# Pooled attention and a squared-ReLU MLP on one core: the attention's score eviction, its normalisation and its query pooling are dealt out anew over ScalarE, VectorE and GpSimd

## The chip, the core and the metric

The kernel runs on one core of one Trainium2 chip. The metric is device time in microseconds (us) of one execution, as the median of several. Five engines work side by side and meet at semaphores: TensorE (PE in the profile; its weight loads are PEld), VectorE (DVE), ScalarE (ACT), GpSimd (POOL) and SyncE (SP, which only issues DMAs here). Each works through its own list of instructions in order.

## The reference

```
q, k, v: (4, 8, 1152, 64) float32;  w_in: (512, 2048);  w_out: (2048, 512)
q_pool = q.reshape(B, H, 576, 2, 64).mean(axis=3)
scores = q_pool @ k.T / 8
scores = scores - max(scores, axis=-1)
attn   = exp(scores);  attn = attn / (sum(attn, axis=-1) + 1e-9)
x      = (attn @ v) with heads side by side: (2304, 512)
h      = maximum(x @ w_in, 0)
out    = (h * h) @ w_out
```

## The kernel before

**Attention.** There are 32 heads, worked on as 16 pairs `n`; a pair is cut into two halves `e` of 288 pooled queries (`NH`). One (pair, half) is the unit of work. Its scores are computed transposed, in nine chunks `c` of 128 keys (`scores`, six matmuls a chunk, into a PSUM buffer `s` of two banks). VectorE moves each chunk to SBUF and takes its maximum on the way (`evict`, L355). After the ninth chunk the nine maxima become one per partition (`max_fin`, `pb`, L309), TensorE transposes them (`max_turn`), and VectorE reduces again (`max_rows`, `nb`, L325). ScalarE then takes the exponential in place, three chunks to an instruction (`expo`, L360); a group of three chunks is a tile `p`. GpSimd adds the three tiles, and then the three chunks of the result, so that one chunk is left (`add`, L397: two adds of 1728 elements a partition and two of 576). TensorE sums that over the keys with a matmul by ones (`total`, L404) and multiplies the exponentials by v (`pv`, L375), both into the one PSUM buffer `c` of the pool `cps`. ScalarE copies the sums out (`total_x`, L408), VectorE inverts them (`recip`, L414), ScalarE sums the inverses up for a later check of the range (`spread`, L417), and VectorE multiplies (`pv_x`, L420) into `xt`.

Before a pair's scores stand its loads, the pooling of its queries on GpSimd (`pool_q`, L225 and L227), transposes of k and q on TensorE in four steps `u` (`prep`), and the split of each result in a high part on ScalarE (`prep_high`, L268) and a low part on VectorE (`prep_low`, L273 and L275). PSUM is a ring `sps` of three buffers for scores, transposes and maxima, and `cps`.

**Order.** `plan` gives each piece of work a key from the tables `AT` and `BT` (kept above what it must follow) and sorts by key. The sorted list is the program order of every engine. While the exponentials of one half run, TensorE works on the scores of the next, and on the sums and values of the half before.

**MLP.** The weights come as pairs of 32-bit integers and are turned into float32 by six VectorE instructions (`convert`, L119 to L133), one add on GpSimd (L135) and a split (`split_w`). A weight unit `u` is one block of `w_in` (even) or `w_out` (odd). Units 0 and 1 are converted near the start, 2 and 3 at the end of the attention (`CU` is 4), the rest within the MLP. `split_x` splits tiles of x, `layer1` and `layer2` are the two matmuls; both follow the attention on TensorE.

Of the kernel before, what the change touches and what calls it, by code (L numbers as in the profile page):

```python
# [37 lines left out]
def kernel(  # L38
# [36 lines left out]
    def run(ctx, exact):  # L75
# [89 lines left out]
        with ExitStack() as a:  # L165
# [5 lines left out]
            sps = a.enter_context(tc.tile_pool(name="sps", bufs=3, space=PSUM))  # L171
            cps = a.enter_context(tc.tile_pool(name="cps", bufs=1, space=PSUM))
# [16 lines left out]
            else:  # L189
                PM = [kq.tile([P, 2, NC], F32, name=f"pm{i}") for i in range(2)]  # L190
# [167 lines left out]
            def expo(n, e, g):  # L358
                p = p_[n, e, g]
                nc.scalar.activation(out=p, in_=p, func=ACTF.Exp, bias=NB_[n % 2][:, e:e + 1])  # L360
# [6 lines left out]
            def both(n, e):  # L367
                if (n, e) not in c_:
                    c_[n, e] = cps.tile([P, 2, 512], F32, tag="c", name="c")
                return c_[n, e]  # L370

            def pv(n, e, c):
                t = both(n, e)
                for h in range(2):
                    i = nc.tensor.matmul(out=t[rows(h), 0, :NH], lhsT=ld_["v", n][:, h, c, :],  # L375
                                         rhs=chunk(n, e, c)[:, h], start=(c == 0), stop=(c == NC - 1))
                    if (n, e) in tx_:

                        tc.declare_no_dep(i.ins, tx_[n, e].ins, reason="the sums' bank is read, this writes the other bank")
# [5 lines left out]
            def parts(n, e):  # L385
                return LASTN if (n, e) == LAST else 1
# [19 lines left out]
            def total_x(n, e):  # L406
                r_[n, e] = ld.tile([P, NH], F32, tag="r", name="r", bufs=2)
                tx_[n, e] = nc.scalar.activation(out=r_[n, e], in_=c_[n, e][:, 1, :NH], func=ACTF.Copy,  # L408
                                                 bias=1e-9 if exact else 1e-30, scale=1.0 if exact else 1.0 + 1e-9,
                                                 accum_out=RM[:, 0, 2 * n + e:2 * n + e + 1])  # L410
# [5 lines left out]
            def spread(n, e):  # L416
                nc.scalar.activation(out=JK, in_=r_[n, e], func=ACTF.Copy, accum_out=RM[:, 1, 2 * n + e:2 * n + e + 1])  # L417
# [289 lines left out]
```

## Time and profile before

| | |
|---|---|
| median of 3 runs | 831.65 us (831.32 to 832.45) |
| the profiled execution | 829.95 us, its span 828.1 us |
| busy in the span | PE 765.0, DVE 596.3, ACT 429.8, POOL 455.4 us |
| busy share | PE 92%, DVE 72%, ACT 52%, POOL 55% |
| chain that ended last | PE 47%, POOL 35%, DVE 9%, issue 6% |

An engine's share is its busy time over the whole span. The attention takes roughly the first half and the MLP the second, with other engines busy in each, so the shares of the whole run don't name the limit of either half. A row of the timeline gives start, duration, engine, line, operation, and what is written from what; in square brackets stands how long the engine sat idle before it, and what ended that.

### The profile page before, as it was taken

To read this page: it belongs to the slowest core of one execution; us is meant where nothing else is said; L and a number is where in the kernel's file an instruction comes from. 1 tells how busy PE (TensorE), PEld (TensorE's weight loads), DVE (VectorE), ACT (ScalarE), POOL (GpSimd) and SP (SyncE) were. 2 spreads that over 40 slices of the span, in tenths; PEclk is the share of its full clock that TensorE was granted. 3 is DMA by queue.
4 is the path that set the end of the run, shared out by engine and by line. 5 is a ranking of instruction groups with operands and counts; after the bars stand their busy time and mean duration, and the time that the engine had idled before them with its cause. 6 is when DMAs were issued, how large, how long until landed. Compare 5 with 4: busy or idle time off the path is not lost.

```text
span 828.1 us, 13837 instructions
## 1 busy us (share of the span) xinstructions
PE 765.0 (92%) x5366; PEld 558.6 (67%) x5366; DVE 596.3 (72%) x1215; ACT 429.8 (52%) x636; POOL 455.4 (55%) x225
## 2 busy tenths in 40 slices
PE   4899999999999999997698999999999999999996
PEld 3665556555555556553476878888888888888885
DVE  5998988888888888885888699685555745445323
ACT  1565566566565566555455745454435444445431
POOL 2699999999999999999245234222112121110000
PEclk9999999999999999998899999999999999999999
DMA  9223323332223323120022112101111010000113
GB/s 246 63 58 87 86 60 87 86 87 60 76 67 87 86 63 83 30 81 0 27 77 76 52 52 77 51 28 50 51 35 42 27 46 31 1 2 26 51 52 105
DMA packets 62090, 50.78 MB, mean 61 GB/s; under 512 B 39232, under 2 KB 49472, under 8 KB 62016
## 3 DMA queue, kind: packets, MB, share of 16 engines
q1 hardware_dynamic: 60576, 47.46, 20.4%
q10 hardware_dynamic: 1440, 2.36, 0.9%
q8 instruction: 44, 0.72, 0.4%
q14 instruction: 30, 0.25, 0.1%
HBM read 45.09 MB, written 4.72 MB: 60 GB/s over the span
## 4 chain that ended last, share of the span: by engine, by line
PE 47%; POOL 35%; DVE 9%; issue 6%; ACT 1%; DMA 1%; SPq 1%; POOLq 0%; DVEq 0%; ACTq 0%
POOL ts L397 31%; PE o L614 22%; PE h L578 20%; PE c L375 3%; POOL qp L225 2%; DVE p L355 2%; PE s L344 2%; DVE xlo L158 1%; DVE h L127 1%; DVE a L124 1%; DVE r L133 1%; DMA raw<-in_moe_w_in_dram 1%; POOL r L135 1%; POOL ql L227 1%; DVE gl L586 1%
## 5 line engine op out<-in xcount | busy, mean ns | idle before, releaser
L355 DVE TENSOR_SCALAR_CACHE_REDUCE p<-s 128x576 f32<-128x576 f32 x288 | 205.0, 754 | 20.6 <-PE s L344 19.0
L578 PE MATMUL h<-xhi,wi 128*128 128x512 f32 (+1 forms) x600 | 174.1, 375 | 5.9 <-ACT wi L145 5.7
L360 ACT ACTIVATE p<-p,nb 128x1728 f32<-128x1728 f32 x96 | 159.8, 1728 | 27.9 <-DVE nb L325 27.9
L614 PE MATMUL o<-wo,gh 128*128 128x512 f32 x540 | 169.7, 395 | 0.9 <-DVE part L622 0.9
L375 PE MATMUL c<-p,vt 128*64 128x288 f32 x1152 | 169.1, 418 | 0.7 <-DVE xt L420 0.7
L344 PE MATMUL s<-qq,kk 64*128 64x288 f32 x1728 | 157.5, 315 | 9.9 <-DVE p L355 7.8
L135 POOL TENSOR_TENSOR r<-r,h 128x512 f32<-128x512 f32 x32 | 47.0, 1470 | 212.7 <-DVE r L133 212.7
L344 PEld LDWEIGHTS s<-qq,kk 64*128 64x128 f32 x1728 | 124.6, 191 | 58.2 <-DVE p L355 30.0
L578 PEld LDWEIGHTS h<-xhi,wi 128*128 128x128 f32 x600 | 110.6, 190 | 29.1 <-ACT wi L145 5.9
L397 POOL TENSOR_TENSOR ts<-p 128x1728 f32<-128x1728 f32 x32 | 123.5, 3859 | 8.0 <-ACT p L360 8.0
L397 POOL TENSOR_TENSOR ts<-ts,p 128x1728 f32<-128x1728 f32 x32 | 125.0, 3908 | 2.5
L586 DVE TENSOR_TENSOR gl<-g,gh 128x512 fp32r<-128x512 f32 (+1 forms) x80 | 54.0, 675 | 96.9 <-ACT gh L585 96.6
L614 PEld LDWEIGHTS o<-wo,gh 128*128 128x128 f32 x540 | 100.3, 188 | 24.5 <-issue 1.3
L578 PE MATMUL h<-xlo,wi 128*128 128x512 f32 (+1 forms) x300 | 111.6, 372 | 0.0
L375 PEld LDWEIGHTS c<-p,vt 128*64 128x64 f32 x1152 | 74.6, 137 | 53.7 <-issue 16.2
L614 PE MATMUL o<-wo,gl 128*128 128x512 f32 x270 | 106.6, 395 | 0.0
L397 POOL TENSOR_TENSOR ts<-ts 128x576 f32<-128x576 f32 x63 | 89.3, 1418 | 4.9
L158 DVE TENSOR_TENSOR xlo<-xt,xhi 128x1024 fp32r<-128x1024 f32 (+7 forms) x40 | 59.3, 1495 | 32.3 <-ACT xhi L157 28.8
L414 DVE RECIPROCAL r<-r 128x144 f32<-128x144 f32 x64 | 64.8, 1035 | 23.3 <-ACT r L408 23.3
L580 ACT ACTIVATE r<-h 128x512 f32<-128x512 f32 (+1 forms) x80 | 44.3, 554 | 71.0 <-PE h L578 71.0
L585 ACT CAST gh<-g 128x512 fp32r<-128x512 f32 (+1 forms) x80 | 46.3, 579 | 54.4 <-PE o L614 48.7
L622 DVE TENSOR_TENSOR part<-part,o 128x512 f32<-128x512 f32 x72 | 48.7, 686 | 21.8 <-PE o L614 21.2
(73 smaller groups left out, 759.3 us busy)
## 6 DMA issues: line engine op xcount, KB each, us to landing
kt<-in_k_dram SPq DMA_DIRECT2D x32, 288.0 KB, 4.1
vt<-in_v_dram SPq DMA_DIRECT2D x16, 576.0 KB, 3.9
qt<-in_q_dram SPq DMA_DIRECT2D x16, 512.0 KB, 3.9
raw<-in_moe_w_in_dram SPq DMA_DIRECT2D x16, 512.0 KB, 3.8
raw<-in_moe_w_out_dram SPq DMA_DIRECT2D x16, 512.0 KB, 3.3
out_dram<-part ACTq DMA_DIRECT2D x18, 128.0 KB, 3.3
out_dram<-part SPq DMA_DIRECT2D x18, 128.0 KB, 2.8
ql<-in_q_dram SPq DMA_DIRECT2D x16, 64.0 KB, 3.7
```

What stands on the lines that cost most here:

```text
L135: nc.gpsimd.tensor_tensor(out=r, in0=r, in1=h.bitcast(F32), op=ALU.add)
L158: nc.vector.tensor_tensor(out=l, in0=x, in1=h, op=ALU.subtract)
L344: nc.tensor.matmul(out=s[:, h, :NH], lhsT=l[rows(h)], rhs=r[rows(h)], start=(i == 0), stop=(i == len(terms) - 1))
L355: nc.vector.tensor_scalar(out=room(n, e, c), in0=s_.pop((n, e, c))[:, :, :NH], scalar1=1.0, scalar2=None, op0=ALU.mult, op1=ALU.max, accum ...
L360: nc.scalar.activation(out=p, in_=p, func=ACTF.Exp, bias=NB_[n % 2][:, e:e + 1])
L375: i = nc.tensor.matmul(out=t[rows(h), 0, :NH], lhsT=ld_["v", n][:, h, c, :], rhs=chunk(n, e, c)[:, h], start=(c == 0), stop=(c == NC - 1))
L397: nc.gpsimd.tensor_tensor(out=t[:, o], in0=t[:, o] if x is None else p_[n, e, x], in1=t[:, y] if isinstance(y, slice) else p_[n, e, y], op ...
L414: nc.vector.reciprocal(out=x, in_=x)
L578: nc.tensor.matmul(out=h, lhsT=w, rhs=x, start=(m == 0), stop=(m == len(mm) - 1))
L586: nc.vector.tensor_tensor(out=gl, in0=g, in1=gh, op=ALU.subtract)
L614: nc.tensor.matmul(out=acc[i][t], lhsT=g, rhs=w, start=(first and m == 0), stop=(last and m == 2))
L622: nc.vector.tensor_tensor(out=y, in0=y, in1=acc[i][t], op=ALU.add)
```

## The change

- Of the nine chunks, 3, 4 and 5 (one tile `p`) are copied out of PSUM by ScalarE. Their maximum is taken by one VectorE reduction over the tile in SBUF (`max_copied`). The chunks run in the order 0, 3, 1, 4, 2, 5, 6, 7, 8.
- The exponential of a tile is two instructions of 864 elements in place of one of 1728.
- All PSUM use of the attention is one ring of four buffers; `c` is taken from it.
- The sums are inverted as exp(-ln(sum)) on ScalarE, with one Newton step of two VectorE instructions, the first of which writes over the sums in PSUM. `recip` and `spread` are gone; a third ScalarE instruction reads the sums for the range check.
- The second half of each pair leaves two chunks to the matmul by ones (three adds on GpSimd, twice the matmuls); the last half of all leaves three (two adds).
- The queries are pooled by VectorE reductions.
- `AT` and `BT` have new values: units 0 and 1 are converted among the work of the first two pairs, the conversions of units 2 and 3 stand among the last attention work, and their loads and those of v in other places.

```diff
-            sps = a.enter_context(tc.tile_pool(name="sps", bufs=3, space=PSUM))
-            cps = a.enter_context(tc.tile_pool(name="cps", bufs=1, space=PSUM))
+            sps = a.enter_context(tc.tile_pool(name="sps", bufs=4, space=PSUM))
...
-                nc.gpsimd.tensor_tensor(out=qp.rearrange("p r h d -> p h r d"), in0=qt[:, :, :, 0, :],
-                                        in1=qt[:, :, :, 1, :], op=ALU.add)
-                nc.gpsimd.tensor_tensor(out=QL[0:NL], in0=ql[:, :, 0, :], in1=ql[:, :, 1, :], op=ALU.add)
+                for h in range(2):
+                    nc.vector.tensor_reduce(out=qp[:, :, h], in_=qt[:, h].rearrange("p r e d -> p r d e"), op=ALU.add, axis=AX.X)
+                nc.vector.tensor_reduce(out=QL[0:NL], in_=ql.rearrange("p h e d -> p h d e"), op=ALU.add, axis=AX.X)
...
+            ORDER = [0, 3, 1, 4, 2, 5, 6, 7, 8]
+            XS = 2
...
             def evict(n, e, c):
-                nc.vector.tensor_scalar(out=room(n, e, c), in0=s_.pop((n, e, c))[:, :, :NH], scalar1=1.0, scalar2=None,
-                                        op0=ALU.mult, op1=ALU.max, accum_out=PM[n % 2][:, e, c:c + 1])
+                x, y = s_.pop((n, e, c))[:, :, :NH], room(n, e, c)
+                if c // G == 1:
+                    nc.scalar.copy(out=y, in_=x)
+                    return
+                i = c if c < G else c - G
+                nc.vector.tensor_scalar(out=y, in0=x, scalar1=1.0, scalar2=None, op0=ALU.mult, op1=ALU.max,
+                                        accum_out=PM[n % 2][:, e, i:i + 1])
+
+            def max_copied(n, e):
+                nc.vector.tensor_reduce(out=PM[n % 2][:, e, NC - G:], in_=p_[n, e, 1], op=ALU.max, axis=AX.XYZ)
...
-                    c_[n, e] = cps.tile([P, 2, 512], F32, tag="c", name="c")
+                    c_[n, e] = bank()
...
-                return LASTN if (n, e) == LAST else 1
+                return LASTN if (n, e) == LAST else 1 + e
...
+                tx_[n, e] = [
+                    nc.scalar.activation(out=r, in_=t, func=ACTF.Ln, bias=SMALL),
+                    nc.scalar.activation(out=r, in_=r, func=ACTF.Exp, scale=-1.0, accum_out=RM[:, 1, k:k + 1]),
+                    nc.scalar.activation(out=JK, in_=t, func=ACTF.Copy, accum_out=RM[:, 0, k:k + 1]),
+                    nc.vector.scalar_tensor_tensor(out=t, in0=t, scalar=1e-30, in1=r, op0=ALU.add, op1=ALU.mult),
+                    nc.vector.scalar_tensor_tensor(out=r, in0=t, scalar=2.0, in1=r, op0=ALU.subtract, op1=ALU.mult),
+                ]
...
-                nc.vector.tensor_tensor(out=x_part(n, e), in0=c_.pop((n, e))[:, 0, :NH], in1=r_.pop((n, e)), op=ALU.mult)
+                    nc.vector.scalar_tensor_tensor(out=x, in0=c, scalar=-1.0, in1=r, op0=ALU.mult, op1=ALU.mult)
...
-            LASTN = 2
+            LASTN = int(BT["lastn"])
...
-            nc.scalar.activation(out=warm, in_=warm, func=ACTF.Exp)
+            nc.scalar.preload_act_table_set("natural_log_exp_and_others")
```

What the new keys do to the order is shown at three places. First ScalarE in the middle of the attention, one half before (`r` are the sums, `kk` and `qq` the high parts of k and q, `p` the exponentials in place):

```order
L268 ACTIVATE kk_104<-s 128x128
L268 ACTIVATE qq_108<-s 128x384
L408 ACTIVATE r,rm<-c 128x288
L417 ACTIVATE jk,rm<-r 128x288
L360 ACTIVATE p<-p,nb_114 128x1728 x3
```

And the same engine there in the changed kernel, from the sums of a second half on (L360 is now the copy of a score chunk, L371 the exponential, L425 to L427 the three instructions on the sums):

```order
L268 ACTIVATE kk_99<-s 128x512
L425 ACTIVATE r<-s,small 128x288
L426 ACTIVATE r,rm<-r 128x288
L427 ACTIVATE jk,rm<-s 128x288
L371 ACTIVATE p<-p,nb_112 128x864 x2
L360 COPY p<-s 128x576 x3
L371 ACTIVATE p<-p,nb_112 128x864 x2
L268 ACTIVATE kk_101<-s 128x512
L371 ACTIVATE p<-p,nb_112 128x864
```

The copies of the next half's chunks now stand between the exponentials of this one. In that list there is one table load ahead of all attention work, and none between the Ln and the Exp.

VectorE in the same stretch before (`pb`, `nb` are the two steps of the maximum, `xt` the product):

```order
L414 RECIPROCAL r<-r 128x144 x2
L309 TENSOR_REDUCE pb_113<-pm_111 128x1
L325 TENSOR_REDUCE nb_115<-s 128x1
L355 TENSOR_SCALAR p,pm_110<-s 128x576 x6
L420 TENSOR_TENSOR xt_82<-c,r 128x288
L355 TENSOR_SCALAR p,pm_110<-s 128x576 x3
```

And in the changed kernel (L367 is `max_copied`, L429 and L430 the Newton step, L226 and L227 the pooling, L442 the product, L363 the eviction):

```order
L367 TENSOR_REDUCE pm_108<-p 128x1
L273 TENSOR_TENSOR kk_100<-s,kk_99 128x512
L309 TENSOR_REDUCE pb_110<-pm_108 128x1
L429 SCALAR_TENSOR_TENSOR s<-s,r 128x288
L430 SCALAR_TENSOR_TENSOR r<-s,r 128x288
L325 TENSOR_REDUCE nb_112<-s 128x1
L226 TENSOR_REDUCE qp<-qt 128x4x64 x2
L227 TENSOR_REDUCE ql<-ql 64x128
L442 SCALAR_TENSOR_TENSOR xt_80<-s,r 128x288
L363 TENSOR_SCALAR p,pm_107<-s 128x576 x6
```

The Newton step now stands between `pb` and `nb`, and the pooling between `nb` and the product.

VectorE at the end of the attention in the changed kernel (L120 to L134 are one unit's conversion, here of unit 2; before, all of it stood behind the last product but one):

```order
L367 TENSOR_REDUCE pm_108<-p 128x1
L120 TENSOR_SCALAR a<-raw 128x512
L309 TENSOR_REDUCE pb_110<-pm_108 128x1
L429 SCALAR_TENSOR_TENSOR s<-s,r 128x288
L430 SCALAR_TENSOR_TENSOR r<-s,r 128x288
L325 TENSOR_REDUCE nb_112<-s 128x1
L122 TENSOR_SCALAR a<-a 128x512
L442 SCALAR_TENSOR_TENSOR xt_83<-s,r 128x288
L125 TENSOR_SCALAR a<-a 128x512
L128 SCALAR_TENSOR_TENSOR h<-raw,a 128x512
L132 TENSOR_SCALAR a<-h 128x512
```

Here the conversion has moved ahead, in between the last half's maximum and the last products.

## Rows read from the trace of the kernel before

**Rows 1.** Chain that ended last, shares of the span by engine.

```profile
PE 47%; POOL 35%; DVE 9%; issue 6%; ACT 1%; DMA 1%; SPq 1%; POOLq 0%; DVEq 0%; ACTq 0%
```

**Rows 2.** Windows: stretch, length; busy PE, PEld, DVE, ACT, POOL; clock; DMA.

```profile
100.33:123.56 23.23, 21.56 (x220) 13.58 (x220) 20.17 (x52) 14.08 (x20) 22.76 (x12) 1.00 0.30 78
...
408.50:414.60 6.10, 5.85 (x23) 4.80 (x24) 6.10 (x10) 3.41 (x6) 0.00 (x0) 0.68 0.16 54
...
455.00:812.00 357.00, 356.11 (x1615) 290.87 (x1615) 210.34 (x310) 169.66 (x276) 67.23 (x46) 1.00 0.13 41
```

**Rows 3.** Timeline of GpSimd over one pair.

```profile
306.42 2.92 POOL L397 TENSOR_TENSOR ts<-ts 128x576 f32<-128x576 f32 x2
309.31 3.85 POOL L397 TENSOR_TENSOR ts<-p 128x1728 f32<-128x1728 f32 x1
...
320.10 1.27 POOL L225 TENSOR_TENSOR qp<-qt 128x512 f32<-128x512 f32 x1
...
321.75 3.86 POOL L397 TENSOR_TENSOR ts<-p 128x1728 f32<-128x1728 f32 x1
```

**Rows 4.** Groups by shape, 100 to 355 us: count, busy us, mean ns, idle before.

```profile
L360 ACT ACTIVATE p<-p,nb 128x1728 f32<-128x1728 f32 x66 | 109.9, 1729 | 18.2 <-DVE nb L325 18.2
L414 DVE RECIPROCAL r<-r 128x144 f32<-128x144 f32 x44 | 44.7, 1036 | 11.6 <-ACT r L408 11.6
...
L268 ACT ACTIVATE kk<-s 128x512 fp32r<-128x512 f32 x22 | 12.0, 595 | 4.1 <-PE s L236 4.1
...
L420 DVE TENSOR_TENSOR xt<-c,r 128x288 f32<-128x288 f32 x22 | 10.0, 452 | 0.0
L417 ACT ACTIVATE jk<-r 128x288 f32<-128x288 f32 x22 | 9.8, 444 | 39.6 <-DVE pb L309 23.0 <-DVE r L414 16.6
...
L325 DVE TENSOR_REDUCE nb<-s 128x1 f32<-128x128 f32 x22 | 6.4, 289 | 6.5 <-PE s L236 6.5
...
L268 ACT ACTIVATE kk<-s 128x128 fp32r<-128x128 f32 x11 | 3.0, 277 | 5.7 <-PE s L236 5.7
L309 DVE TENSOR_REDUCE pb<-pm 128x1 f32<-128x9 f32 x22 | 2.8, 127 | 0.0
```

**Rows 5.** Groups of the whole run: eviction copy on ScalarE, a low part on VectorE.

```profile
L620 ACT COPY part<-o 128x512 f32<-128x512 f32 x18 | 10.2, 590 | 0.2
...
L146 DVE TENSOR_TENSOR wi<-r,wi 128x512 fp32r<-128x512 f32 x1 | 0.7, 678 | 0.0
```

**Rows 6.** Timeline: three exponentials in a row, and a score chunk up to its eviction.

```profile
349.74 5.00 ACT L360 ACTIVATE p<-p,nb 128x1728 f32<-128x1728 f32 x3 [1.29 <-DVE nb L325]
...
210.52 0.83 PEld L344 LDWEIGHTS s<-qq,kk 64*128 64x128 f32 x12 [0.44 <-DVE nb L325]
...
211.22 0.76 DVE L355 TENSOR_SCALAR_CACHE_REDUCE p<-s 128x576 f32<-128x576 f32 x1 [0.25 <-PE s L344]
```

**Rows 7.** Timeline 388 to 398 us: a GpSimd add, and VectorE beside such adds.

```profile
388.00 3.83 POOL L397 TENSOR_TENSOR ts<-p 128x1728 f32<-128x1728 f32 x1
...
390.88 1.51 DVE L146 TENSOR_TENSOR wf<-r,wf 128x512 fp32r<-128x512 f32 x1
...
396.43 1.51 DVE L121 TENSOR_SCALAR a<-a 128x512 f32<-128x512 f32 x1
```

**Rows 8.** Timeline at the start: first two evictions, exponentials of the second pair's second half.

```profile
19.58 0.75 DVE L355 TENSOR_SCALAR_CACHE_REDUCE p<-s 128x576 f32<-128x576 f32 x1
...
20.25 0.75 DVE L355 TENSOR_SCALAR_CACHE_REDUCE p<-s 128x576 f32<-128x576 f32 x1
...
58.24 5.00 ACT L360 ACTIVATE p<-p,nb 128x1728 f32<-128x1728 f32 x3 [0.34 <-DVE nb L325]
```

**Rows 9.** Timeline at the end of the attention: last exponentials, first use of unit 2.

```profile
381.66 4.99 ACT L360 ACTIVATE p<-p,nb 128x1728 f32<-128x1728 f32 x3 [0.36 <-DVE nb L325]
...
408.55 0.29 PEld L578 LDWEIGHTS h<-xhi,wi 128*128 128x128 f32 x1 [5.88 <-ACT wi L145]
...
410.19 0.58 PE L578 MATMUL h<-xhi,wi 128*128 128x256 f32 x1 [0.20 <-DVE wi L146]
```

More of the change, by code (lines that the diff above doesn't have):

```diff
@@ L189, in run @@
             else:
-                PM = [kq.tile([P, 2, NC], F32, name=f"pm{i}") for i in range(2)]
+                PM = [kq.tile([P, 2, NC - G + 1], F32, name=f"pm{i}") for i in range(2)]
                 PB = [kq.tile([P, 2], F32, name=f"pb{i}") for i in range(2)]
@@ L376, in pv @@
                                          rhs=chunk(n, e, c)[:, h], start=(c == 0), stop=(c == NC - 1))
-                    if (n, e) in tx_:
-                        tc.declare_no_dep(i.ins, tx_[n, e].ins, reason="the sums' bank is read, this writes the other bank")
+                    for d in tx_.get((n, e), ()):
+                        tc.declare_no_dep(i.ins, d.ins, reason="works on the sums' bank, this writes the other bank")
             def x_part(n, e):
@@ L406, in total_x @@
             def total_x(n, e):
[L407 to L410, printed above, removed]
+                r = r_[n, e] = ld.tile([P, NH], F32, tag="r", name="r", bufs=2)
+                t = c_[n, e][:, 1, :NH]
+                if exact:
+                    tx_[n, e] = [nc.scalar.activation(out=r, in_=t, func=ACTF.Copy, bias=1e-9)]
+                    return
+                k = 2 * n + e
+                tx_[n, e] = [
[5 more added lines that the diff above has]
+                ]
             def recip(n, e, i):
@@ L454, in plan @@
                         at(t, ("prep", n, u), prep, n, u, after=[("pq", n), ("lk", n)])
[L455 to L456 removed]
+                        at(t + (A[f"h{u}"] if n > 1 else .05), ("hi", n, u), prep_high, n, u, after=[("prep", n, u), ("s", n - 2, 1, NC - 1)])
+                        at(t + (A[f"l{u}"] if n > 1 else .1), ("lo", n, u), prep_low, n, u, after=[("hi", n, u)])
@@ L457, in plan @@
                     if n < NP - 1:
-                        at(base + A["pq"], ("pq", n + 1), pool_q, n + 1, after=[("lq", n + 1)] + [("prep", n, u) for u in range(4)])
+                        at(base + A["pq"] if n else BT["pq"], ("pq", n + 1), pool_q, n + 1, after=[("lq", n + 1)] + [("prep", n, u) for u in range(4)])
                     for e in range(2):
                         cy = base + e
-                        for c in range(NC):
-                            t = cy + .1 + (.05 + A["ss"]) * c + A[f"S{e}0"] + (BT[f"s{e}"] if n == 0 else 0)
+                        for i, c in enumerate(ORDER):
+                            t = cy + .1 + (.05 + A["ss"]) * i + A[f"S{e}0"] + (BT[f"s{2 * n + e}"] if n < 2 else 0)
@@ L463, in plan @@
                             at(t, ("s", n, e, c), scores, n, e, c, after=[("lo", n, u) for u in range(4)])
-                            at(t + .06 + A["e"], ("ev", n, e, c), evict, n, e, c, after=[("s", n, e, c)])
-                        t = cy + 1 + A[f"m{e}"] + (BT[f"s{e}"] if n == 0 else 0)
-                        at(t - .02, ("mf", n, e), max_fin, n, e, after=[("ev", n, e, c) for c in range(NC)])
+                            at(t + .06 + A["ea" if c // G == 1 else "e"], ("ev", n, e, c), evict, n, e, c, after=[("s", n, e, c)])
@@ L488, in plan @@
                             values()
-                        for i in range(2):
-                            at(t + A[f"rc{e}{i}"], ("rc", n, e, i), recip, n, e, i, after=[("tx", n, e), ("rc", n, e, i - 1)])
-                        at(t + A[f"rm{e}"], ("rm", n, e), spread, n, e, after=[("rc", n, e, 1)])
-                        at(t + A[f"px{e}"], ("px", n, e), pv_x, n, e, after=[("rc", n, e, 1), ("pv", n, e, NC - 1)])
+                        at(t + A[f"px{e}"], ("px", n, e), pv_x, n, e, after=[("tx", n, e), ("pv", n, e, NC - 1)])
                 last = 2 * NP
@@ L495, in plan @@
                     if u >= EARLY:
-                        at(last - 2 + u / 2, ("lr", u), load_raw, u, after=[("cv", u - 2, NCV - 1)])
+                        at(4 + u / 2, ("lr", u), load_raw, u, after=[("cv", u - 2, NCV - 1)])
                     t = BT[f"c{u}"] + (0 if u < EARLY else last)
```

53 lines of the change are left out of this document (30 added, 23 removed).

## The prediction

> **What bounds the kernel now.** I read the chain first, because the busy shares are means over two unlike halves. TensorE and GpSimd hold most of it [rows 1]: two limits, one after the other. The windows show where. A pair of the attention takes 23.23 us, of which GpSimd is busy 22.76, TensorE 21.56, VectorE 20.17 and ScalarE 14.08; in the MLP from 455 us on TensorE is busy 356.11 of 357.00 [rows 2]. GpSimd's timeline says what it does in that pair: the four adds of a half take from 309.31 to 320.10, 10.79 us, of which each small add is 1.46, and the pooling of the next queries 1.65 more [rows 3]. So the attention is bound by GpSimd, and from 455 us on nothing in this change touches the limit: the time moves only by what moves the attention's end and the first 50 us of the MLP.
>
> **GpSimd.** The pooling goes (1.65) and one small add of the two halves' eight (1.46). What is left is 2 x 10.79 - 1.46 = 20.1 us a pair. GpSimd stops being the limit if anything else needs more.
>
> **ScalarE** had 14.08 busy a pair, and gets three things. Exponentials: three of 1728 elements take 5.00 us [rows 6], the last of them 1.73 [rows 4], so they start 1.64 apart and overlap by 0.09. An element costs (595 - 277) / 384 = 0.83 ns by the two sizes of kk [rows 4]. Half an exponential is then 1.73 - 864 x 0.83 ns = 1.01, or 0.92 apart: 12 x 0.92 - 6 x 1.64 = +1.2. Copies: 512 elements out of PSUM take 0.590 [rows 5], 576 take 0.64, or 0.55 in a row: six are +3.3. The sums take three instructions instead of two, one more like L417's 0.44 [rows 4], and the Exp can't overlap the Ln whose result it reads: +1.1 for two halves. The new sum is 19.7 us.
>
> **VectorE** loses six evictions (they start 0.67 apart [rows 8]: 4.0) and four half reciprocals (1.036 [rows 4], some 0.08 of it under the next: 3.8). It gains two maxima over 1728 elements, four Newton instructions and the pooling. The trace has no large reduction out of SBUF. If it went two elements a cycle it would be near 1.0 us, at one element (about 1.04 ns, as 576 take 0.67 and more) 1.9; the reductions there are, 128 elements in 0.289 [rows 4], are nearest to one, and I take 1.87. A Newton instruction has the shape of L420, 0.452 [rows 4], bounded by 0.3 if only the elements count and 0.6 if PSUM as output costs more. The pooling is 512 elements twice and 256 once, 1.55 together. 20.17 - 4.0 - 3.8 + 3.7 + 1.8 + 1.55 = 19.4. TensorE gets two matmuls more a pair, some 0.5, but fewer changes between scores and values, so at most 22.1.
>
> **Waits.** Four engines between 19.4 and 22.1 do not give a pair of 20, since each works in order. I followed one pair through the order of the changed kernel. ScalarE's list is the ring that closes last, and three waits stand in it. (1) In a second half, behind its three instructions on the sums, the next exponential needs `nb`, and VectorE runs the two Newton instructions before `nb`: 2 x 0.46 + 0.29 + handoffs = 1.4 us in which ScalarE has nothing. In the first half an exponential and two high parts stand there, so it costs nothing. (2) Then two exponentials and the copy of chunk 3 are done 2.5 us after `nb`. Chunk 4 comes later: `nb` is followed on VectorE by the pooling and the product (2.0), which gives the fourth PSUM buffer back; chunk 1 takes it (half of the 0.83 that two chunks' weight loads take), then chunk 4 runs, and its result is 0.70 behind its start [rows 6]: 3.25. That is 0.75 of waiting. (3) Chunk 5 behind the transposes of q, 0.4. So 19.7 + 1.4 + 0.75 + 0.4 = **22.25 us a pair**, 2 us over GpSimd. GpSimd's adds end 0.5 us ahead of the sums' matmul in that walk, so it is close behind.
>
> **Sharing of VectorE and GpSimd.** A subtraction of two SBUF tiles on VectorE took 1.51 us at 390.88 and ended 0.56 behind the GpSimd add that had run to 391.83 [rows 7]; the same alone takes 0.678 [rows 5]. A conversion step with one SBUF input, L121, took 1.51 there as well. The small reduction `pb` takes 127 ns on average though GpSimd is busy 98% of the stretch [rows 2, 4]. So some instructions of VectorE wait for a running GpSimd add to end, and reductions don't. The Trainium skill (SBUF — State Buffer, Who interferes with whom) says it so: VectorE instructions with two SBUF inputs, or in a two-port mode, and GpSimd's lock each other out for a whole instruction, reductions never do. Both rows agree with it. That speaks against this change at one point: the conversions of units 0 and 1 leave the free start and stand among GpSimd's adds, and those of 2 and 3, two low parts and one `xlo` come before the last adds. An add is 3.85, so a wait is from 0 to 3.85; by the share of time an add has left to run I take 1.5 each.
>
> **The sum**, between marks that both kernels have. (a) Start: the first eviction comes at about 12 us instead of 19.58, since no conversion stands ahead. Twelve conversion instructions with their waits are paid within two pairs instead, and each first pair runs at the new ring's rate, where before GpSimd's backlog was still filling. In my walk the exponentials of the second pair's second half, 58.24 before [rows 8], come at 66.4: **+8.2**. (b) From there to the last half's exponentials (381.66 [rows 9]) are 14 pairs, 23.10 each: 14 x (22.25 - 23.10) = **-11.9**. (c) Low parts and `xlo` in the last two pairs, less what has no next pair to prepare: **+3.9**. (d) From the last exponentials to the first matmul with unit 2's low part at 410.19 were 28.5 us [rows 9]. In the walk the sums' matmul of the last half is done 16.4 behind (two adds instead of three), unit 2's high part 2.6 later, its low part 22.4 behind, as unit 3's conversion stands ahead of it on VectorE: **-6.1**. (e) TensorE waited 5.88 there and then had a clock of 0.68 for 6.1 us [rows 9, 2]; without the wait it keeps the clock: 2 us, and 1 us for conversions already done: **-3**. Together -8.9. Against the profiled execution's own 829.95 that is 821.1; the median lies 1.7 higher, so between the two **822 us**.
>
> **Rivals.** A measurement of this kernel tells about 0.2% from no change.
> *The ring is shorter.* If the handoffs of (1) to (3) cost half, and copies slip under exponentials, GpSimd's 20.1 with some slack decides: 20.7 a pair, 14 x 1.55 less than forecast, **800 us**. For it: VectorE and ScalarE have 2.5 to 3 us to spare. Against it: the order puts the Newton step ahead of `nb`.
> *Slower: ScalarE's ring is longer than GpSimd's was.* If short instructions don't overlap as the long ones do, 18 of them a pair cost 0.09 more: 23.9 a pair, +23, **845 us**. It decides from 22.9 a pair on, where the 14 pairs no longer pay for (a) and (c). Against it: the long ones do overlap [rows 6]. For it: four engines within 2 us, and every handoff I priced at nothing adds.
> *The conversions wait for whole adds.* 17 instructions wait 3.85 instead of 1.5, half of them where nothing else is late: +20, **842 us**. It decides from half a us each.
> *The last half comes no earlier and the MLP's start is bound by VectorE anyway* ((d) and (e) give nothing): **831 us**, no change.
>
> **Numbers.** Forecast 0.47, shorter ring 0.22, longer ring 0.16, conversions 0.09, no change 0.06. The forecast's own spread is 0.5 us a pair, 7 us, so 812 to 829, all of it faster; the conversions' rival reaches down into no change. Faster 0.71, same 0.07, slower 0.22. The range from 800 to 838 cuts off the lower part of the shorter ring and most of the slower two.
>
> **What would show it.** The mean pair between 100 and 300 us is 22.25, with GpSimd at 90% and ScalarE near 88%, its idle time in front of L371 (`nb`) and of L360 (scores). A maximum over 1728 elements at 1.9 us, not stretched by GpSimd; an exponential near 1.0. The conversion steps of the first two units stretched to well over a us where a GpSimd add runs. No TensorE wait of 5 us ahead of unit 2. The prediction is wrong if the pair is under 21.3 or over 22.9, or if the second pair's mark is more than 5 us from 66.4.

## The result and the profile after

The changed kernel takes **803.68 us** (median of 4 runs, 803.09 to 805.01) against 831.49 of the kernel before on the same chip: ratio 0.9666, 95% interval 0.9649 to 0.9683. 27.8 us are gained where 9.5 were forecast. The profiled execution has a span of 803.2 us.

The windows after, the columns as in [rows 2]: one pair of the attention, the attention's end, the MLP.

```profile
100.50:121.59 21.09, 20.29 (x226) 14.79 (x224) 19.55 (x45) 19.05 (x34) 19.85 (x7) 1.00 0.35 85
361.00:382.00 21.00, 15.14 (x103) 7.88 (x98) 19.06 (x18) 8.39 (x16) 16.72 (x7) 0.84 0.13 39
440.00:800.00 360.00, 355.00 (x1604) 289.34 (x1602) 208.03 (x308) 163.16 (x264) 64.58 (x44) 1.00 0.14 43
```

A pair takes 21.09 us instead of 23.23, and no engine is busy all of it: TensorE 20.29 us, GpSimd 19.85, VectorE 19.55, ScalarE 19.05. Next, GpSimd's timeline over one such pair, which answers to [rows 3].

```profile
196.06 3.88 POOL L408 TENSOR_TENSOR ts<-p 128x1728 f32<-128x1728 f32 x1 [0.36 <-ACT p L371]
...
205.93 3.90 POOL L408 TENSOR_TENSOR ts<-p 128x1728 f32<-128x1728 f32 x1 [0.49 <-ACT p L371]
...
213.88 2.93 POOL L408 TENSOR_TENSOR ts<-ts 128x576 f32<-128x576 f32 x2
217.15 3.88 POOL L408 TENSOR_TENSOR ts<-p 128x1728 f32<-128x1728 f32 x1 [0.34 <-ACT p L371]
```

The first add of each half now waits for exponentials (0.36, 0.49). ScalarE's timeline of the second half:

```profile
208.03 0.50 ACT L425 ACTIVATE r<-s,small 128x288 f32<-128x288 f32 x1
208.56 0.45 ACT L426 ACTIVATE r<-r 128x288 f32<-128x288 f32 x1
...
209.01 0.39 ACT L427 ACTIVATE jk<-s 128x288 f32<-128x288 f32 x1
...
210.71 1.93 ACT L371 ACTIVATE p<-p,nb 128x864 f32<-128x864 f32 x2 [1.22 <-DVE nb L325]
213.04 1.38 ACT L360 COPY p<-s 128x576 f32<-128x576 f32 x2 [0.41 <-PE s L344]
214.61 0.64 ACT L360 COPY p<-s 128x576 f32<-128x576 f32 x1 [0.20 <-PE s L344]
```

So ScalarE waits 1.22 for `nb` (L325) and 0.61 for scores (L344). The chain of waits through one pair shows what closes the loop (start, length, what was waited on; VectorE's maximum over the copied chunks is L367, the transpose L236, the products with the values L386):

```profile
184.48 1.35 DVE p L363 x4
185.83 1.86 DVE pm L367
...
188.51 0.27 PE s L236 x2
188.78 2.09 PE s L386 x16
190.87 2.63 PE s L344 x36
...
193.52 0.64 ACT p L360
194.16 1.82 ACT p L371 x2
...
198.33 0.39 ACT jk L427 x2
...
202.77 1.18 ACT p L360 x2
203.94 0.29 ACT qq L268
...
204.80 2.11 DVE p L363 x5
```

It goes VectorE, TensorE, ScalarE (193.52 to 204.23, half of the pair), VectorE again, and does not touch GpSimd. It is a loop: from the start of the maximum at 185.83 to the end of the last evictions at 206.91, where the next maximum can start, are 21.08 us, the whole pair, and each piece starts within 0.6 us of the end of the one before.

**Where the time went**, by the marks of the prediction:

| stretch | before | after | change | forecast |
|---|---|---|---|---|
| (a) to the exponentials of the second pair's second half | 58.24 | 61.45 | +3.2 | +8.2 |
| (b) 14 pairs (before: their mean; after: the steady pair) | 14 x 23.10 = 323.4 | 14 x 21.09 = 295.3 | -28.1 | -11.9 |
| (c) what the 14 pairs take beyond that | 0 | 299.84 - 295.3 = 4.6 | +4.6 | +3.9 |
| (d) last exponentials to the first use of unit 2's low part | 28.5 | 361.29 to 385.55: 24.3 | -4.2 | -6.1 |
| (e) the rest, from the span (828.1, 803.2) | 417.9 | 417.65 | -0.3 | -3.0 |

The error lies in (b), 16.2 us beyond the forecast; all else together is 0.3 us off, because errors of either sign cancel. The changes add up to -24.8, as the two profiled executions (829.95 and 805.01 us) do, where the medians differ by 27.8. A steady pair before took 23.22 by GpSimd's adds, a little over the mean of 23.10. In (d), 385.55 is the start of the group of matmuls in which that part is first used.

### The profile page after: what moved, and what is told of

Its sections match the earlier page's. It is cut to its first block, busy times and chain, and to the rows that moved or that the text cites. A ratio compares the mean times of both kernels' runs of the same rounds, so it can differ in the third digit from the quotient of the medians.

```text
span 803.2 us, 13958 instructions
## 1 busy us (share of the span) xinstructions
PE 748.0 (93%) x5430; PEld 579.4 (72%) x5430; DVE 600.0 (75%) x1103; ACT 510.0 (63%) x859; POOL 409.9 (51%) x177
## 3 DMA queue, kind: packets, MB, share of 16 engines
q1 hardware_dynamic: 60576, 47.46, 21.3%
## 4 chain that ended last, share of the span: by engine, by line
PE 63%; DVE 15%; ACT 15%; issue 3%; POOL 2%; DMA 1%; SPq 0%; DVEq 0%; POOLq 0%
PE o L637 24%; PE h L601 22%; ACT p L371 8%; PE s L344 8%; PE s L386 7%; DVE p L363 5%; DVE pm L367 4%; ACT p L360 3%; POOL ts L408 1%; DVE xlo L159 1%; ACT kk L268 1%; PE s L236 1%; PE s L415 1%; ACT qq L268 1%; ACT r L426 1%
## 5 line engine op out<-in xcount | busy, mean ns | idle before, releaser
L371 ACT ACTIVATE p<-p,nb 128x864 f32<-128x864 f32 x192 | 184.0, 1011 | 26.0 <-DVE nb L325 26.0
L386 PE MATMUL s<-p,vt 128*64 128x288 f32 x1152 | 154.1, 413 | 0.0
L136 POOL TENSOR_TENSOR r<-r,h 128x512 f32<-128x512 f32 x32 | 49.1, 1534 | 203.4 <-DVE r L134 203.4
L363 DVE TENSOR_SCALAR_CACHE_REDUCE p<-s 128x576 f32<-128x576 f32 x192 | 138.4, 755 | 12.1 <-PE s L344 6.4
L344 PE MATMUL s<-qq,kk 64*128 64x288 f32 x1728 | 136.7, 308 | 5.6 <-DVE xt L442 1.4
L344 PEld LDWEIGHTS s<-qq,kk 64*128 64x128 f32 x1728 | 123.3, 193 | 21.7 <-issue 12.7
L386 PEld LDWEIGHTS s<-p,vt 128*64 128x64 f32 x1152 | 85.5, 139 | 50.4 <-issue 2.9
L159 DVE TENSOR_TENSOR xlo<-xt,xhi 128x1024 fp32r<-128x1024 f32 (+7 forms) x40 | 61.0, 1542 | 33.6 <-ACT xhi L158 30.3
L360 ACT COPY p<-s 128x576 f32<-128x576 f32 x96 | 59.7, 641 | 19.1 <-PE s L344 17.1
L408 POOL TENSOR_TENSOR ts<-ts 128x576 f32<-128x576 f32 x47 | 69.0, 1468 | 3.7
L158 ACT CAST xhi<-xt 128x1024 fp32r<-128x1024 f32 (+7 forms) x40 | 45.9, 1152 | 31.8 <-PE h L601 30.9
```

The source lines that it names most:

```text
L136: nc.gpsimd.tensor_tensor(out=r, in0=r, in1=h.bitcast(F32), op=ALU.add)
L159: nc.vector.tensor_tensor(out=l, in0=x, in1=h, op=ALU.subtract)
L344: nc.tensor.matmul(out=s[:, h, :NH], lhsT=l[rows(h)], rhs=r[rows(h)], start=(i == 0), stop=(i == len(terms) - 1))
L360: nc.scalar.copy(out=y, in_=x)
L363: nc.vector.tensor_scalar(out=y, in0=x, scalar1=1.0, scalar2=None, op0=ALU.mult, op1=ALU.max, accum_out=PM[n % 2][:, e, i:i + 1])
L408: nc.gpsimd.tensor_tensor(out=t[:, o], in0=t[:, o] if x is None else p_[n, e, x], in1=t[:, y] if isinstance(y, slice) else p_[n, e, y], op ...
```

## The experiments

Unless it says otherwise an edit is made in the changed kernel (803.68 us, pair 21.09). "Pair" is the distance of two first adds of the same half on GpSimd in that run's timeline, one trace a run; where one figure stands, most pairs lie within 0.05 of it. The medians are of 4 to 10 runs; the ratio is to the kernel before on the same chip (medians 830.9 to 831.8).

| run | us | ratio to before, 95% | pair |
|---|---|---|---|
| a_nonewton | 803.03 | 0.9653 (0.9622 to 0.9684) | 21.10 |
| a_nb_both | 813.66 | 0.9794 (0.9768 to 0.9820) | 21.87 |
| a_parts1 | 886.83 | 1.0666 (1.0638 to 1.0693) | 27.3 to 27.7 |
| a_parts1b | 811.98 | 0.9776 (0.9757 to 0.9796) | 21.62 |
| a_parts2 | 804.60 | 0.9688 (0.9667 to 0.9709) | 21.30 |
| a_poolq | 835.18 | 1.0044 (1.0030 to 1.0058) | 22.5 to 24.5 |
| a_noterm | 796.98 | 0.9585 (0.9567 to 0.9603) | 20.80 |
| a_noterm_nonewton | 794.99 | 0.9547 (0.9526 to 0.9567) | 20.81 |
| a_peplus | 807.61 | 0.9707 (0.9662 to 0.9753) | 21.23 |
| a_nomax | 800.26 | 0.9624 (0.9605 to 0.9643) | 20.97 |
| a_nocheck | 801.39 | 0.9636 (0.9614 to 0.9659) | 20.99 |
| a_nocopy | 838.66 | 1.0086 (1.0055 to 1.0117) | 23.75 |
| a_unsplit | 829.46 | 0.9974 (0.9955 to 0.9993) | 22.05 |
| b_parts (before, one part) | 814.90 | 0.9803 (0.9786 to 0.9820) | 22.1 |
| b_both (before, two parts) | 850.31 | 1.0212 (1.0188 to 1.0237) | 24.2 to 25.8 |
| b_group (before, three) | 890.06 | 1.0697 (1.0679 to 1.0715) | 26.5 to 27.2 |
| a_convstart | 808.13 | 0.9707 (0.9689 to 0.9726) | 21.10 |
| a_xlate | 805.52 | 0.9687 (0.9671 to 0.9704) | 21.09 |

The interval of the changed kernel is 0.9649 to 0.9683. Those of a_nonewton, a_parts2, a_peplus, a_nocheck and a_xlate overlap it, so by their time these runs are not told from it; what is said of the first four rests on the pair.

### Is it ScalarE's ring, by its wait for nb?

The theory of the prediction was that ScalarE's ring sets the pair; the rival, that GpSimd does. Two runs bring `nb` earlier.

```diff
 a_nonewton, in total_x:
-    nc.vector.scalar_tensor_tensor(out=t, in0=t, scalar=1e-30, in1=r, ...)
-    nc.vector.scalar_tensor_tensor(out=r, in0=t, scalar=2.0, in1=r, ...)
 a_nb_both, VectorE's list:
-    L367 max, L273 kk, L309 pb, L429, L430 (Newton), L325 nb
+    L367 max, L309 pb, L325 nb, L273 kk, L429, L430 (Newton)
```

> The changed kernel without the Newton step: the product takes the result of Ln and Exp as it is, so the output is a little less exact, and that part of the computation is left out. VectorE loses 1.84 us a pair, nb comes 0.35 earlier in both halves, and the product too. Ring theory: pair shorter by 0.35 to 0.6, 14 x 0.5 = -7, about 797 us. GpSimd theory: no change in the pairs, 803 us. If VectorE (19.6 busy of 21.09) were the limit: pair shorter by up to 1.84, but GpSimd's 20.1 stops it at about 1.0: 790 us.

> The changed kernel with one part of VectorE's list in another order: pb, its transpose and nb come right behind the maximum; the low part of kk (0.68) and the two instructions of the Newton step (0.47 and 0.46) come behind nb. nb is then some 0.95 us earlier (0.6 for kk, 0.35 for the part of the Newton step that the transpose does not cover). Ring theory: ScalarE's wait of 1.22 us for nb, once a pair, shrinks to about 0.3, pair 20.2 to 20.5, 14 x 0.75 = -10, about 793 us. GpSimd theory: no change, 804 us. Against both: the PSUM buffers of kk and of the sums come free 1 to 1.5 us later, and scores wait for a buffer instead, +0 to +0.5 a pair, up to 811.

Without the Newton step VectorE has 1.84 us less a pair, and the pair stays at 21.10. ScalarE's wait for `nb` fell and its wait for scores rose by the same; the waits from 100 to 330 us, some 11 pairs (in total, times, longest):

```profile
ACT p L360 <- PE s L344: 12.2, 22, 1.2
...
ACT p L371 <- DVE nb L325: 8.2, 11, 0.8
```

In the changed kernel these were 6.9 and 13.4. So neither VectorE's load as a whole nor this wait for `nb` sets the pair, and the ring theory in this form falls. With the low part of `kk` and the Newton step behind `nb`, the wait for `nb` fell to 5.3, and the pair grew by 0.8: TensorE now waits for PSUM buffers, which come free later.

```profile
ACT p L360 <- PE s L344: 18.2, 24, 1.2
...
PEld s L344 <- ACT p L360: 12.1, 20, 0.6
...
ACT p L371 <- DVE nb L325: 5.3, 11, 0.5
PEld s L344 <- DVE s L434: 4.4, 10, 0.4
```

### Is it GpSimd?

```diff
 def parts(n, e):
-    return LASTN if (n, e) == LAST else 1 + e
+    return LASTN if (n, e) == LAST else 1      # a_parts1, a_parts1b (and a13=0.3)
+    return LASTN if (n, e) == LAST else 2      # a_parts2
 def pool_q(n):                                 # a_poolq: both adds on nc.gpsimd again
```

> The changed kernel with one edit: the sums of every half but the last are kept as one part again, so GpSimd gets the small add back, 1.43 us more a pair in all pairs but the last. Ring theory (the pair of 21.09 us is ScalarE's 19.05 of work and 2.04 of waiting for nb and for scores; GpSimd, 19.86 busy, has 1.2 to spare, 0.84 of it waits for the exponentials): only about 0.2 us a pair shows, 15 x 0.2 = +3, about 807 us, and GpSimd's waits for exponentials go to nearly nothing. GpSimd theory (the pair is GpSimd's adds with a handoff that cannot be hidden, all else has slack): the whole 15 x 1.43 = +21, about 825 us, pair 22.5.

> As the run with one part of the sums, but the small add that comes back keeps its place ahead of the next half's first add (its key is set to 0.3). GpSimd 1.43 us more a pair, TensorE two matmuls less. Ring theory of ScalarE: about 807 us. Loop theory (from the end of GpSimd's adds to TensorE's sums, values and scores, to ScalarE's copies and exponentials, back to GpSimd's adds of the pair after: 42.18 us for two pairs, in which TensorE has 18.8, ScalarE 2.5 and GpSimd 20.75): GpSimd's own list, 20.3 with its gaps, becomes 21.75 a pair and decides, 15 x 0.66 = +10, about 814 us. GpSimd theory, all of the add shows: 15 x 1.43 = +21, 825 us.

> The changed kernel with two parts of the sums in every half: GpSimd one small add less a pair, 1.43 us, TensorE two matmuls more, some 0.35. Loop theory: half of 1.43 - 0.35 a pair, pair 20.55, 15 x 0.54 = -8, about 796 us. Ring theory of ScalarE, and VectorE as the limit: no change, 804 us. TensorE alone as the limit: 15 x 0.35 = +5, 809 us.

> The changed kernel with the pooling of the queries back on GpSimd: GpSimd 1.65 us more a pair, VectorE 1.7 less, right behind nb of a second half, so the product and the evictions behind it come earlier. Loop theory: GpSimd's own list, 20.3 with its gaps, becomes 22.0 a pair, 14 x 0.9 = +13, about 817 us. Ring theory of ScalarE: its wait for scores shrinks, GpSimd at 22.0 decides all the same but from 21.09, so these two do not part here; VectorE as the limit: pair shorter, below 800 us.

a_parts1 did not test its question: the key of the returned add placed it behind the next half's first add (its 1.39 us stand at 111.81, after the add of 108.00), so the sums came late and the pair was over 27. With the key mended, GpSimd works without a gap and is the limit, but 1.43 us more work cost 0.53 a pair. With 1.43 less the pair did not shrink: it grew by 0.21; TensorE has more matmuls for the sums, and they now wait for PSUM buffers that VectorE frees (3.4 us between 100 and 330). GpSimd alone does not set 21.09 either; its own list needs some 20.2, 21.62 less 1.43. The pooling on GpSimd costs 31 us, far beyond its 1.65: there the queries' pooling waits behind a half's adds, and TensorE's transposes wait for it (17.7 us of weight loads waiting for `qp` between 100 and 330). Its place in the order was chosen for VectorE, so 31 us is not the price of the pooling's work alone.

### Is it TensorE?

```diff
 a_noterm:  terms = [kh.qh, kl.qh, kh.ql]  ->  [kh.qh, kl.qh]
 a_peplus:  chunks 6 to 8: terms.append(terms[2])
```

> The changed kernel without the third of the three products that make a chunk of scores (high part of the keys by low part of the queries), which is left out in all halves, so the scores are a little less exact: TensorE 36 matmuls less a pair, 36 x 0.072 = 2.6 us; nothing else changes. Loop theory: the loop is 2 to 2.6 shorter in two pairs, pair 19.9 to 20.1, and GpSimd's own 20.3 stops it: 20.4, 14 x 0.7 = -10, about 794 us. Ring theory of ScalarE: its waits for scores (0.6) go, the wait for nb stays or grows, pair 20.5 to 21.1, 796 to 804 us. GpSimd alone or VectorE as the limit: no change, 804 us.

> The changed kernel with more work on TensorE alone: the third product of the last three chunks of every half is added twice, so their scores are a little off; 12 matmuls more a pair, 12 x 0.072 = 0.86 us. TensorE as the limit of the pair: all of it shows, 15.5 x 0.86 = +13, about 817 us. Ring theory of ScalarE, or GpSimd, with TensorE 0.3 or more below: +0.5 or less a pair, 811 us or less.

> The changed kernel without the third product of the scores and without the Newton step (both left out, so the output is a little less exact): TensorE 2.6 us less a pair, VectorE 1.84 less, nb 0.35 earlier. Without the third product alone the pair was 20.80. If the ring of ScalarE and VectorE through nb closes there: pair 20.45, 14 x 0.35 = -5, about 792 us. If GpSimd's list (20.3 with its gaps) and a handoff that is not hidden (0.6 a pair) close there: no change to that run, 797 us.

2.6 us less on TensorE gave 0.29 a pair, 0.86 more cost 0.14, and VectorE's 1.84 less on top gave nothing. TensorE alone is not it. What closes at 20.80 can be read from a_noterm's timelines: the first add of a pair starts at 119.73 and the next one at 140.54. Between them GpSimd's four adds end at 130.58, TensorE has the sums, 24 values and the transpose of `pb` (130.62 to 134.44), VectorE `nb`, and ScalarE three exponentials, three copies and a high part up to the next exponential.

```profile
119.73 3.88 POOL L408 TENSOR_TENSOR ts<-p 128x1728 f32<-128x1728 f32 x1 [0.62 <-ACT p L371]
...
134.48 0.29 DVE L325 TENSOR_REDUCE nb<-s 128x1 f32<-128x128 f32 x1 [0.27 <-PE s L236]
...
134.81 2.83 ACT L371 ACTIVATE p<-p,nb 128x864 f32<-128x864 f32 x3
...
140.54 3.87 POOL L408 TENSOR_TENSOR ts<-p 128x1728 f32<-128x1728 f32 x1 [0.55 <-ACT p L371]
```

No scores and no Newton step stand in this loop, and a_noterm_nonewton has the same one (118.89 to 139.71). By then each engine's list by itself had been ruled out, which left loops through several. Two runs take one link each out of the chain shown in the result.

```diff
 a_nomax:   L367, the maximum over the copied chunks, is not made
 a_nocheck: L427, the copy that sums the sums for the range check, is not made
```

> The changed kernel without the maximum over the three copied chunks (left out: the bias of the exponentials is taken from six chunks of nine): VectorE 1.86 us less in each half, directly ahead of pb. The chain of one pair, 21.09 long, goes from VectorE's evictions and this maximum to pb, to TensorE's transpose, 16 products with the values and 36 with the scores, to ScalarE's copies, exponentials and sums, to VectorE's low part of q and back to the evictions; the maximum of the second half stands in it with 1.86. If this mixed loop sets the pair: it falls to what closes next, 20.8 or a little less, 14 x 0.3 to 0.5 = -4 to -7, 797 to 800 us. If it is only the engines' lists (VectorE 1.84 less by the Newton step gave nothing): 804 us.

> The changed kernel without the copy that sums the sums for the range check (left out: the range check), ScalarE some 0.4 us less in each half, one of them in the chain of a pair between Exp and the next exponential. If the mixed loop sets the pair: 0.29 (where the next limit stands, 20.8) to 0.4 less, 14 x 0.3 to 0.4 = -4 to -6, 798 to 800 us. If ScalarE's work has slack, as its waits for nb and for scores suggest: 804 us.

Both shorten the pair, by 0.12 and 0.10, where the Newton step, twice 0.9 us of VectorE's work but behind `pb`, gave nothing. The size is below what was expected: another loop closes first. The chain of a_nomax goes through GpSimd, whose next first add (last row, from its timeline) waits for the first of those exponentials:

```profile
123.67 3.91 POOL ts L408
...
130.63 0.71 PE s L415 x4
131.34 2.91 PE s L386 x24
...
136.05 2.23 PE s L344 x30
...
139.06 0.64 ACT p L360
139.70 2.74 ACT p L371 x3
...
140.69 3.87 POOL L408 TENSOR_TENSOR ts<-p 128x1728 f32<-128x1728 f32 x1 [0.49 <-ACT p L371]
```

The add before it in the loop started at 119.72, 20.97 earlier. So there are three loops close together: one of 21.09 through VectorE, TensorE and ScalarE, one of 20.97 through GpSimd, TensorE with the scores, and ScalarE, and, without 2.6 us of TensorE's work, the one of 20.80 through GpSimd, TensorE, `nb` and ScalarE. L427 stands in neither of the last two, which fits the 20.99 of a_nocheck. Each was followed in one trace.

### What the parts that cost work bring

```diff
 a_nocopy:  def evict: no nc.scalar.copy, VectorE evicts all nine; no maximum L367
 a_unsplit: XS = 2  ->  XS = 1
```

> The changed kernel with the copies undone: VectorE evicts all nine chunks with its running maximum, the maximum over the copied chunks goes (VectorE 6 x 0.68 more, 2 x 1.86 less a pair, so about the same), ScalarE loses six copies, some 3.3 us a pair; four PSUM buffers stay. Ring theory: ScalarE's work falls to 15.8 a pair and its waits for scores go; the pair falls to what GpSimd lets through, about 20.3, 14 x 0.8 = -11, about 792 us; it stays there only if nb is not later than now. GpSimd theory: no change, 804 us. A third, that the copies are what pays because nine evictions in a row make nb late: nb comes up to 2 us later in a half, pair 22 to 23, 816 to 830 us.

> The changed kernel with each exponential in one instruction of 1728 elements again: ScalarE 1.2 us less work a pair, but the sums' three instructions now stand behind a whole exponential. TensorE as the limit (20.3 busy and 0.8 of waits of 21.09): no change, 804 us, plus what a later start of the sums costs, up to +0.3 a pair, 808. Ring theory of ScalarE: pair shorter by up to 1.0, 790 us.

Both take work from ScalarE, and both lose the gain: the copies undone cost 35 us, the exponentials in one piece 26. Unsplit, ScalarE's two exponentials (3.37 us) stand ahead of the copies, and TensorE's next transposes wait for the buffer that a copy frees:

```profile
149.34 3.37 ACT L371 ACTIVATE p<-p,nb 128x1728 f32<-128x1728 f32 x2 [0.68 <-DVE nb L325]
...
152.61 1.16 ACT L360 COPY p<-s 128x576 f32<-128x576 f32 x2
...
153.28 0.28 PE L236 MATMUL s<-ident,qp 64*128 64x64 f32 x2 [1.17 <-ACT p L360]
```

From 100 to 330 us the loads for the transposes wait 15.4 us in this way (3.0 in the changed kernel), and ScalarE waits 28.9 for `nb` (13.4); how the 26 us divide between the two was not tested. Without the copies ScalarE waits 30.3 us in 9 places for a transposed k and 21.5 for `nb` in the same stretch, and TensorE's weight loads wait 28.3 for VectorE's evictions, a wait that the changed kernel's list does not have. These prices hold for the changed kernel's order; whether another order would need the copies was not tried.

### What GpSimd's relief gives in the kernel before

```diff
 b_parts: parts 1  ->  1 + e
 b_both:  and pool_q on nc.vector
 b_group: and vs=0.025  ->  vs=-0.035 (values in one block)
```

> The kernel before with one part of the change alone: the sums of each second half are kept as two parts, so GpSimd has one small add less a pair (1.46 us; 22.76 busy becomes 21.3), TensorE two matmuls more. GpSimd as the limit before, with nothing close behind: pair 23.23 - 1.46 = 21.8, 14 x 1.4 = -20, about 811 us. TensorE close behind (21.56 busy a pair, 0.35 more, and 0.8 of handoffs as in the changed kernel): pair 22.7, 14 x 0.5 = -7, about 824 us.

> The kernel before with the whole of GpSimd's relief and nothing else: two parts of the sums in each second half, and the pooling on VectorE. GpSimd 19.6 us a pair, VectorE 20.17 + 1.55 = 21.7, TensorE as in the run with the two parts alone, whose pair was 22.1 with TensorE busy 99% of it. TensorE as the limit from there on: pair 22.1 again, about 815 us. GpSimd: pair 20.5, 792 us. VectorE with its handoffs: 22.5 or more, 820 us or more.

> The same, and the products with the values stand in one block of TensorE's list instead of between the scores, in threes and fours. In the trace of before four of them between scores start 0.16 apart and in a block 0.128, scores in twelves 0.083 and in a block of 54 0.072: a change there and back costs about 0.28, seven such changes fewer a pair are 2.0 us. TensorE as the limit, and its changes as what the changed kernel saves: pair 21.0 at the least if VectorE (21.7) allows it, so 21.7 to 22.0, 809 to 813 us. If the evictions starve while the block runs: 22.5 or more, 820 us or more.

One small add less gave 16.9 us, over half of the whole change's gain: the kernel before was bound by GpSimd, as [rows 2, 3] say. It stops at 22.1 us, where TensorE is busy 228.36 of 230.00 us (GpSimd 223.04):

```profile
100.00:330.00 230.00, 228.36 (x2334) 145.06 (x2330) 207.68 (x529) 146.88 (x197) 223.04 (x96) 1.00 0.29 79
```

The other two miss. In the old order the pooling on VectorE makes ScalarE and GpSimd wait (4.05 us ahead of the add at 133.16), and with the values in one block as well the pair is about 27. They say nothing on TensorE's list, only that these parts do not pay without the new order. What TensorE saves in the changed kernel is read from timelines alone: here of b_parts, products with the values between scores.

```profile
137.11 0.71 PE L375 MATMUL c<-p,vt 128*64 128x288 f32 x4
137.75 1.06 PE L344 MATMUL s<-qq,kk 64*128 64x288 f32 x12
138.74 0.71 PE L375 MATMUL c<-p,vt 128*64 128x288 f32 x4
```

Four values take 0.64 to the next start and twelve scores 0.99. In the changed kernel, 24 values in a row take 3.01 (196.28 to 199.29) and 54 scores 3.71 (211.89 to 215.60), so 0.50 and 0.82 for as many: by these rows a change there and back costs about 0.31. The values of a pair stand in nine blocks in b_parts and in four in the changed kernel; five changes fewer are 1.6 us, and TensorE's busy time fell by as much, from 21.9 to 20.3 a pair. The Trainium skill (TensorEngine Tiling (Array Packing), Key Properties) says that a change of tiling mode drains TensorE; the rows name 128*64 for the values and 64*128 for the scores, and the 0.31 us agree in kind.

### The start and the end

```diff
 a_convstart: c0=1.996, c1=2.91             ->  c0=-19.269, c1=-19.2
 a_xlate:     x=-1.193, w0=-0.88, w1=-1.431 ->  x=1.713, w0=0.334, w1=2.305
```

> The changed kernel with the twelve conversion instructions of units 0 and 1 back at the start, ahead of the first eviction, as before. The first eviction then comes at about 19.6 us instead of 11.9. If the spread conversions cost what their stretched durations show in the changed kernel (work 6.7 and some 5 of waiting for GpSimd's adds, most of it late for nb), the mark of the second pair's exponentials stays within 2 us of 61.45: 802 to 806 us. If they hide behind other work there: the mark comes 6 to 8 later, 811 us. If their waits cost more than their work, as the 1.5 us each of the prediction has it: the mark comes 2 to 4 earlier, 800 us.

> The changed kernel with the two low parts of wf and the first xlo late again, by the keys that they had before: they no longer stand among the adds of the last pair but one. If these three are the whole of the 4.6 us by which the 14 pairs are longer than 14 x 21.09: the last exponentials come at 357 instead of 361.3. What follows then decides: they have to be done ahead of the MLP, where VectorE has the last conversions; if they fit in its waits there, 799 to 800 us; if they are late for the first matmuls of the MLP, 804 us or more.

With the conversions at the start the first eviction comes at 26.12, 14.2 later than in the changed kernel, since the raw weights land only at 18.70, and the mark moves by 7.0 to 68.47. If the later start carries through in full, the spread conversions cost the start 14.2 - 7.0 = 7.2 us. In the changed kernel they take 11.3 us in all (groups on VectorE, 15 to 70 us):

```profile
L134 DVE SCALAR_TENSOR_TENSOR r<-raw,a 128x512 f32<-128x512 uint32 x2 | 3.0, 1490 | 0.0
L122 DVE TENSOR_SCALAR a<-a 128x512 f32<-128x512 f32 x2 | 2.5, 1248 | 0.0
L120 DVE TENSOR_SCALAR a<-raw 128x512 int32<-128x512 int32 x2 | 1.9, 962 | 0.0
L132 DVE TENSOR_SCALAR a<-h 128x512 int32<-128x512 int32 x2 | 1.6, 815 | 0.0
```

Unhindered they would take 6.2 (the four steps of the kind of L120 0.43 each, the other two 0.69): 5.1 us of waiting in twelve instructions, 0.4 each.

a_xlate is not told from the changed kernel. Its last exponentials came later, at 363.98: a moved low part waits for another add (3.05 at 355.79), and the last `nb` for it (ScalarE waits 5.95).

## Why the prediction was right and wrong

**Right:** the sign; that GpSimd bounded the attention (b_parts) and TensorE the MLP; the single costs (an exponential of 864 elements 1.01 us, 0.92 apart; a copy 0.64; the large maximum 1.95, a Newton instruction 0.46); that the first eviction would come at about 12 (11.90).

**The step that failed is the pair of 22.25 us**, "ScalarE's list is the ring that closes last". The pair is 21.09, under the 21.3 below which the prediction called itself wrong. As a sum it was 19.7 of work and 1.4 + 0.75 + 0.4 of waits. Measured on ScalarE: 19.05 busy and 2.04 idle, of which 1.22 for `nb` and 0.61 for scores. So the work was forecast 0.65 too long and the waits 0.51. Some 0.4 of the 0.65 less work lies in the sums: they had 2.1 a pair and I added 1.1 for a third instruction, but the three take 1.4 a half (208.03 to 209.49), as the copy (209.01) starts beside the read of the Exp's sum (208.91, 0.18 long). And the second and third wait were half of what I walked through (0.61 for 1.15). 14 x 1.16 is 16.2 us, the whole error of the sum. The reason given for the ring was wrong too: `nb` earlier did not shorten the pair (a_nonewton), nor does any one engine's list set it. What sets it is the loop of 21.09 through VectorE, TensorE and ScalarE, with one through GpSimd 0.12 us behind (a_nomax, a_nocheck). The wait for `nb` that I priced first stood in neither. TensorE, which I bounded by 22.1 a pair, was busy 20.29; at 22.1 no pair of 21.09 would have been possible.

**What the edits do.** I counted the copies and the halved exponentials as 4.5 us of ScalarE's work a pair. Undone, they cost 35 and 26 us, and the waits that come with it say that a chunk of scores, or a transpose, then gets its PSUM buffer later. A price by work alone gave them the wrong sign.

**The rivals.** The shorter ring came nearest in its time (20.7 a pair, 800), but that is luck in part: it had GpSimd's list decide, which needs only 20.2. The longer ring did not occur. Conversions do wait for GpSimd's adds, 0.4 each where 1.5 was taken, which with the faster pair is why (a) is 5.0 short: 61.45 is just inside the 5 us given. In the last pairs they wait longer than forecast, here on VectorE's timeline:

```profile
361.17 2.95 DVE L122 TENSOR_SCALAR a<-a 128x512 f32<-128x512 f32 x1
...
367.52 3.95 DVE L132 TENSOR_SCALAR a<-h 128x512 int32<-128x512 int32 x1
```

**(d) and (e)** gave 4.5 instead of 9.1. TensorE waits for the sums of the half before the last, and has the values of both halves behind them, so the last sums are done 19.1 us behind the last exponentials, not 16.4. And the wait of 5.88 ahead of unit 2 is gone, but not its time: it comes back as 3.61 ahead of the first layer, and as 4.76 twenty us later (1.81 at that place before), behind ScalarE, which waits 4.10 for a conversion.

```profile
366.99 1.23 PE L415 MATMUL s<-ts,one 128*64 128x288 f32 x4 [4.29 <-POOL ts L408]
368.01 9.28 PE L386 MATMUL s<-p,vt 128*64 128x288 f32 x58
...
384.05 0.47 PE L601 MATMUL h<-xhi,wf 128*128 128x256 f32 x2 [3.61 <-DVE xt L442]
...
404.19 1.22 PE L637 MATMUL o<-wf,gh 128*128 128x512 f32 x2 [4.76 <-ACT part L643]
```

The clock was kept where the first layer starts (1.00 from 384 to 395), but not around it: it was 0.79 from 368 to 378, behind the wait of 4.29, and 0.52 from 404.19 to 410, behind the wait of 4.76, so there it stood at the lower of its two levels (1.2 of 2.4 GHz).

**What stays open:** how much of the gain behind b_parts is TensorE's fewer changes and how much the earlier buffers; the two runs meant for that missed, and none took the fourth PSUM buffer or the new order away alone. No run that leaves nothing out was faster than the changed kernel.

## What to carry to other kernels

When four engines are each busy for nine tenths of the time or more, add up loops, not lists: follow one buffer or one result from engine to engine until it comes back, and compare that length with the pair. Work that is moved to an engine with room, or cut in pieces, is priced by what it lets start earlier, not only by its duration. And a relief of the engine that bounds a stage is worth only the distance to the next one: here 1.46 us off GpSimd gave 1.1 a pair, and TensorE, busy 99% of it, stood there.

## What the runs showed of the hardware

A conversion of 512 elements took up to 3.95 us beside GpSimd's adds and 0.43 alone, and an add beside it 4.30 instead of 3.88. The conversion that took 3.95 (367.52 to 371.47) ended 0.28 behind the add of 4.30 (366.89 to 371.19). The Trainium skill (SBUF — State Buffer, Who interferes with whom) calls the port pair that VectorE shares with GpSimd an exclusive lock; these rows agree. The wait was 0.4 us in the mean near the start and up to 3.5 at the end of the attention. That the three ScalarE instructions of 288 elements on the sums, two of them with an accumulated sum, take 1.36 us up to the start of the next (197.26 to 198.62) was not expected, nor was the 0.31 us of a change between values and scores on TensorE.
